# Weight-gradient stores: three half tiles in w1's place for one full tile, and four small rows on GpSimd's queue

## The chip, the cores and the metric

The kernel runs on one core of a Trainium2 chip. The core has five engines that run side by side, each in the order of its own instruction stream: TensorE (PE, with its weight loads shown as PEld), VectorE (DVE), ScalarE (ACT), GpSimd (POOL) and SyncE (SP). Sixteen DMA engines move data between the chip's memory (HBM) and the core's working memory (SBUF); transfers are put on queues by SP, ACT and POOL. Matrix products land in PSUM, of eight banks. The metric is the device time of one execution in microseconds (us), lower is better. Before the change it is 919.31 us, the median of 6 runs (916.63 to 921.01).

## The reference

The reference is one decode step of a transformer block and its gradients. Two sequences (B = 2), one token each, D = 640, 32 heads of 128, caches of 4,096 positions, an MLP with 1,728 hidden units, all in bfloat16.

```python
def _fwd_reference(A_x, A_k_cache, A_v_cache, A_wq, A_wo, B_x, B_w1, B_w2):
    # _A_ref: q = x @ wq; p = softmax(q k^T * Dh**-0.5); o = p v; return o @ wo
    # _B_ref: relu(x @ w1) @ w2
    x = A_x
    h = x + _A_ref(_layernorm(x, axis=-1), A_k_cache, A_v_cache, A_wq, A_wo)
    h2 = h + _B_ref(_layernorm(h, axis=-1), B_w1, B_w2)
    return h2

def reference(...):
    _out, _vjp = jax.vjp(_f, A_x, A_k_cache, A_v_cache, A_wq, A_wo, B_w1, B_w2)
    return (_out, *_vjp(grad_out))
```

There are eight outputs. out_0 is the block's output and out_1 the gradient of x (2 rows of 640 each). out_2 and out_3 are the gradients of the K and V caches, 64 MiB each: per head an outer product of a column over 4,096 positions and a row of 128. out_4 to out_7 are the gradients of wq, wo, w1 and w2: each is a sum of two outer products (one per sequence), 14.9 MB together.

## The kernel before, in words

There are 64 pairs of sequence and head. A first pass (p1_iter) loads K and V of each pair in tiles of 1 MiB (128 partitions of 8 KiB) and makes scores, softmax and attention output. A second pass (p2_iter) needs V once more (tile Wt), makes the gradient of the softmax with it, and writes two outer products of 1 MiB, gK and gV, on VectorE (L829); POOL issues their stores (L867, L886). One call of p2_iter is a turn here; it can be counted by its activation rb (L856). A turn consists of seven steps. In the second half of the second pass there is no first pass beside it.

Beside the turns run three background generators in a fixed program order: bg (the MLP, then go_group, which makes the gradient at the attention output for a group of heads, then mlp_out), bg2 (fin_gen, the weight gradients) and bg3 (gx_gen, the gradient of x). The Python code that builds the program gives each a credit per step (0.65 for bg2), and each `yield` says what a piece costs; nothing is decided at run time. Each engine executes its own instructions in the order in which they were built.

SBUF is handed out in tiles of 8 KiB per partition with tags: "ld" for loads, "g" for gK and gV, "q" for weights late in the kernel, "f" for weight gradients under way. take() gets a tile of a tag and give() brings it back; share() sets how many each tag is to own, and a tile that comes back goes to a tag that owns too few. rested(tag, n) is true when the tag's next tile was given back at least n steps ago. Twelve tiles exist from the start; more come when pools that are no longer needed are released. When the MLP no longer needs w1 (17,280 bytes per partition), its place goes to the pools fin (small tiles of the weight gradients) and big2 (one tile of 8 KiB, tag "f"). Until turn 36 this is the only "f" tile; from then on share() wants three.

outer_rows makes a weight gradient. For each row k of a group and each piece of up to 512 columns, PE makes an outer product into a PSUM tile o_ps (L933), ScalarE copies it into the tile ot (L939), and when the tile is full ScalarE issues its store (L941). One tile holds 4,096 elements per partition: six rows of 640 or two of 1,728 or 2,048. Before it takes a tile, outer_rows waits for rested("f", 13). The order is out_7, out_6, out_5 in two halves, out_4 in two halves.

store_row (L644 on) turns one row of out_0 or out_1 by PE, copies it on VectorE into orow and issues a DMA of 5 x 128 elements, on SP's queue (L651). SP issues the loads of Wt (L458), wqs (L975) and w2 (L361) in program order on the same queue. gx_gen uses a tile gxj of 2 KiB per partition in fin as the place for products that nobody reads.

Of the kernel before, what the change touches and what calls it, by code (L numbers as in the profile page):

```python
# [8 lines left out]
BF16 = mybir.dt.bfloat16  # L9
# [6 lines left out]
def kernel(  # L16
# [20 lines left out]
    nc = tc.nc  # L37

    B, Sq, D = A_x.shape
    _, H, Sk, Dh = A_k_cache.shape  # L40
# [25 lines left out]
    cols = ctx.enter_context(tc.tile_pool(name="cols", bufs=1))  # L66
# [6 lines left out]
    def pst(shape, dtype, role, name):  # L73

        k = banks[role].pop(0)
        banks[role].append(k)
        return ps.tile(shape, dtype, tag=f"bank{k}", bufs=1, name=name)


    NBIG = 12  # L80
    homes = {"ld": list(range(NBIG)), "g": [], "f": [], "q": []}
    free = {tag: len(v) for tag, v in homes.items()}
    owned = dict(free)
    wanted = {}
    pools = [big] * NBIG
# [3 lines left out]
    def take(tag, shape, name):  # L89
        assert free[tag] > 0, (tag, name)  # L90
        free[tag] -= 1
        k = homes[tag].pop(0)
        t = pools[k].tile(shape, BF16, tag=f"big{k}", bufs=1, name=name)
        home_of[id(t)] = (tag, k, t)
        return t

    def goes_to(tag):

        if owned[tag] > wanted.get(tag, len(pools)):
            for other in homes:  # L100
                if owned[other] < wanted.get(other, 0):
                    return other
        return tag

    def give(t, to=None):
        tag, k, _ = home_of.pop(id(t))
        to = to or goes_to(tag)
        owned[tag] -= 1
        owned[to] += 1
        free[to] += 1  # L110
        homes[to].append(k)
        given_at[k] = step[0]

    def rested(tag, n):

        return free[tag] > 0 and (forced[0] or step[0] >= given_at.get(homes[tag][0], -n) + n)

    def share(**want):

        wanted.clear()  # L120
        wanted.update(want)
        for tag in homes:
            while free[tag] > 0 and goes_to(tag) != tag:
                to = goes_to(tag)
                homes[to].append(homes[tag].pop(0))
                for d in (free, owned):
                    d[tag] -= 1
                    d[to] += 1

    def more_home(tag, pool):  # L130
        homes[tag].append(len(pools))
        pools.append(pool)
        free[tag] += 1
        owned[tag] += 1
# [6 lines left out]
    def wait(n):  # L141

        end = step[0] + n * spread[0]
        while step[0] < end and not forced[0]:
            yield 0.0
        yield
# [493 lines left out]
    def spread_cols(t, colsrc, n):  # L640

        for c in range(n):
            nc.tensor.transpose(t[:, c * 128:(c + 1) * 128], colsrc[:, c:c + 1].to_broadcast([128, 128]), ident_bf[:])

    def store_row(col_bf, n, dst):

        t = pst([16, 128], BF16, "mid", "row_ps")
        nc.tensor.transpose(t[0:n, :], col_bf, ident_bf[:])
        r = small.tile([16, 128], BF16, tag="orow", bufs=2, name="orow")
        nc.vector.tensor_copy(out=r[0:n, :], in_=t[0:n, :])  # L650
        nc.sync.dma_start(out=dst, in_=r[0:n, :])  # L651

    def ttr(in0, in1, acc, width, kc=128, junk=None):
        if junk is None:
# [259 lines left out]
    def outer_rows(L, nrow, R, N, out_ap, cc):  # L914


        P = nrow // cc
        grp = max(1, min(cc, 4096 // N))
        out_v = out_ap.rearrange("(p c) n -> p c n", c=cc)
        for c0 in range(0, cc, grp):  # L920
            gn = min(grp, cc - c0)
            while not rested("f", 13):
                yield 0.0
            ot = take("f", [128, grp, N], "ot")
            todo = [(k, n0, min(512, N - n0)) for k in range(gn) for n0 in range(0, N, 512)]
            made = []
            for x in range(len(todo) + 1):
                if x < len(todo):
                    k, n0, nn = todo[x]
                    q = 32 * (fw[0] % 4)  # L930
                    o_ps = pst([128, 512], FP32, "o", "o_ps")
                    fw[0] += 1
                    nc.tensor.matmul(o_ps[0:P, 0:nn], lhsT=L[q:q + B, bass.ds(c0 + k, P, step=cc)],  # L933
                                     rhs=R[q:q + B, n0:n0 + nn], start=True, stop=True)
                    made.append((o_ps, k, n0, nn))
                    yield 0.3
                if x > 0:
                    o_ps, k, n0, nn = made[x - 1]
                    nc.scalar.copy(out=ot[0:P, k, n0:n0 + nn], in_=o_ps[0:P, 0:nn])  # L939
                    yield 0.3  # L940
            nc.scalar.dma_start(out=out_v[:, c0:c0 + gn, :], in_=ot[0:P, 0:gn, :])  # L941
            give(ot)

    def fin_gen(fin):
        FIN["wide"] = [fin.tile([128, 4, 4, 32], BF16, tag="wide", bufs=2, name="wide") for _ in range(2)]
# [23 lines left out]
    def gx_gen(fin):  # L969
        tiles = []  # L970

        def fetch():
            while len(tiles) < ND and free["q"] > 0:
                t = take("q", [128, HD], "wqs")
                nc.sync.dma_start(out=t[:], in_=wq_r[:, len(tiles), :])  # L975
                tiles.append((t, step[0]))

        while not all(("go", B - 1, h) in done for h in range(H)):
            yield 0.0
        while free["q"] < B:  # L980
            yield 0.0
        banks["o"].remove(6)
        banks["gq"] = [6]
        yield from wait(1)
        rows = []
        for b in range(B):
            row = take("q", [128, HD], "gqr")
            for h0 in range(0, H, GH):
                t_ps = pst([128, GH * 128], BF16, "gq", "gq_ps")
                spread_cols(t_ps, GQc[:, h0:h0 + GH, b], GH)  # L990
                nc.scalar.copy(out=row[:, h0 * 128:(h0 + GH) * 128], in_=t_ps[:])
                yield 1.0
            rows.append(row)
        banks["o"].append(6)
        GW = 1024
        NGW = HD // GW
        gxp = fin.tile([128, B, ND, NGW], FP32, tag="gxp", name="gxp")
        junk = fin.tile([128, GW], BF16, tag="gxj", name="gxj")
        for c in range(ND):
            while c >= len(tiles) or (step[0] < tiles[c][1] + 16 and not forced[0]):  # L1000
                fetch()
                yield 0.0
            t = tiles[c][0]
            for b in range(B):
                for k in range(NGW):
                    ttr(t[:, k * GW:(k + 1) * GW], rows[b][:, k * GW:(k + 1) * GW], gxp[:, b, c, k:k + 1], GW, junk=junk)
                    if b == B - 1 and k == NGW - 1:
                        give(t)
                        fetch()
                    yield 0.9  # L1010
        for row in rows:
            give(row)
        gx_bf = fin.tile([128, ND, B], BF16, tag="gxb", name="gx_bf")
        gx1b = fin.tile([128, B, ND], FP32, tag="gx1b", name="gx1b")
        nc.vector.reduce_sum(out=gx1b[:], in_=gxp[:], axis=AX.X)
        yield from ln_bwd(gx1b[:], x1c[:], rstd1[:], gh1c[:], gx_bf[:], B)
        for b in range(B):
            gxo = small.tile([128, ND], BF16, tag="gxo", bufs=2, name="gxo")
            nc.vector.tensor_copy(out=gxo[:], in_=gx_bf[:, :, b])
            yield from wait(2)  # L1020
            store_row(gxo[:], ND, out_1[b].rearrange("s (c p) -> (s c) p", p=128))
            yield
# [94 lines left out]
    fin = big1 = big2 = big3 = None  # L1117
# [12 lines left out]
    for n, (i, j) in enumerate(plan):  # L1130
# [4 lines left out]
        if i is None and plan[n - 1][0] is not None:  # L1135
            pkp.release()
            big1 = tc.alloc_tile_pool(name="big1", bufs=1)
            more_home("ld", big1)
            share(ld=KEPT[1] + 4, g=4)
# [6 lines left out]
        more = int(late[0])  # L1146
        if fin is not None and not bg2 and not bg3:
            share(ld=8 + 3 * more, g=6 + 3 * more)
        elif fin is not None and j >= H + KEPT[1] - 1:
            share(ld=5 + more, g=4 + 2 * more, f=3, q=2 + 3 * more)  # L1150
        if j is not None:
            while g2 is not None:
                p2_step()
# [3 lines left out]
        if i is None and ("w1", 1) in done and fin is None:  # L1157
            wts.release()
            fin = tc.alloc_tile_pool(name="fin", bufs=1)
            big2 = tc.alloc_tile_pool(name="big2", bufs=1)  # L1160
            more_home("f", big2)
            banks.update(sps=[2, 3], o=[4, 5, 6])
            bg2.append(("fin", fin_gen(fin)))
            bg3.append(("gx", gx_gen(fin)))
# [85 lines left out]
```

## Time and profile before

| what | value |
|---|---|
| median of 6 runs | 919.31 us (916.63 to 921.01) |
| the profiled execution | 920.25 us, span 917.9 us |
| PE, DVE, ACT, POOL busy | 745.9, 694.1, 531.4, 167.1 us (81, 76, 58, 18%) |
| bytes moved by DMA | 363.00 MB, mean 395 GB/s |
| queue of the loads (SP), of gK and gV (POOL), of ACT | 212.18, 134.23, 14.91 MB; 57.9, 35.4, 4.1% of 16 engines' span |
| stores of ot | 18, of 432 to 1,024 KB, 323 to 392 ns each to issue, 6.0 to 20.6 us to landing |
| gK and gV stores | 128, 0.53 us each to issue, 5.2 to 30.8 us to landing |
| stores of orow | 4, on SP, 1.2 KB each |
| last instruction of the loop | gK store at 907.4 us |

The span is the time from the first to the last instruction of the profiled execution; its device time lies a little above it. Busy times of engines overlap. A DMA share of 1.0 says that all sixteen engines had packets all the time.

### The profile page before, as it was taken

To read this page: it belongs to the slowest core of one execution; us is meant where nothing else is said; L and a number is where in the kernel's file an instruction comes from. 1 tells how busy PE (TensorE), PEld (TensorE's weight loads), DVE (VectorE), ACT (ScalarE), POOL (GpSimd) and SP (SyncE) were. 2 spreads that over 40 slices of the span, in tenths; PEclk is the share of its full clock that TensorE was granted. 3 is DMA by queue.
4 is the path that set the end of the run, shared out by engine and by line. 5 is a ranking of instruction groups with operands and counts; after the bars stand their busy time and mean duration, and the time that the engine had idled before them with its cause. 6 is when DMAs were issued, how large, how long until landed. Compare 5 with 4: busy or idle time off the path is not lost.

```text
span 917.9 us, 26498 instructions
## 1 busy us (share of the span) xinstructions
PE 745.9 (81%) x11226; PEld 623.5 (68%) x11226; DVE 694.1 (76%) x1291; ACT 531.4 (58%) x1096; POOL 167.1 (18%) x329
## 2 busy tenths in 40 slices
PE   5998998999989898888887827776868799878492
PEld 5887787888878787777776726655757566555362
DVE  4654786877779888777787889878798449998875
ACT  4564554566777777676742626444646667566362
POOL 1222222223201111010011112211122111111111
PEclk9998998999999999999985767555555556565556
DMA  9999999998789999999999999999999999999997
GB/s 346 418 395 410 406 396 409 412 416 338 305 315 332 419 421 422 422 422 421 413 379 425 372 426 397 392 381 411 379 378 386 425 386 425 425 425 425 427 418 301
DMA packets 59478, 363.00 MB, mean 395 GB/s; under 512 B 5696, under 2 KB 15552, under 8 KB 19168
## 3 DMA queue, kind: packets, MB, share of 16 engines
q1 hardware_dynamic: 37920, 212.18, 57.9%
q0 software_dynamic: 18432, 134.23, 35.4%
q10 hardware_dynamic: 3008, 14.91, 4.1%
q8 instruction: 88, 1.44, 0.6%
q14 instruction: 30, 0.25, 0.1%
HBM read 212.16 MB, written 149.13 MB: 394 GB/s over the span
## 4 chain that ended last, share of the span: by engine, by line
PE 37%; DMA 31%; DVE 16%; ACT 8%; issue 6%; POOL 0%; SPq 0%; POOLq 0%; ACTq 0%; DVEq 0%
DMA Vt<-in_A_v_cache_dram 16%; DMA out_dram<-gV 9%; PE t_ps L437 9%; PE m_ps L471 7%; PE t_ps L416 6%; DMA out_dram<-gK 6%; DVE gV L829 4%; ACT t_sb L421 3%; DVE gK L829 3%; PE o_ps L933 3%; PE s_ps L427 3%; DVE junk L656 2%; PE u_ps L500 2%; ACT t_sb L442 2%; PE dp_ps L450 2%
## 5 line engine op out<-in xcount | busy, mean ns | idle before, releaser
L421 ACT COPY t_sb<-t_ps 128x1024 bf16<-128x1024 bf16 x223 | 217.8, 1017 | 49.7 <-PE t_ps L416 49.0
L442 ACT COPY t_sb<-t_ps 128x512 f32<-128x512 f32 x256 | 149.8, 587 | 149.0 <-PE t_ps L437 144.6
L478 DVE TENSOR_TENSOR pk<-Kt,ep 128x2048 bf16<-128x2048 bf16 x128 | 156.4, 1222 | 62.5 <-ACT ep L526 27.1
L437 PE MATMUL t_ps<-ident_f,Wt 128*128 128x128 f32 x848 | 192.6, 374 | 2.6 <-ACT t_sb L421 2.6
L471 PE MATMUL m_ps<-pk,Vt 128*128 128x129 bf16 x2048 | 173.5, 224 | 17.5 <-DMA Vt<-in_A_v_cache_dram 15.9
L829 DVE TENSOR_TENSOR gV<-rb,pp 128x2048 bf16<-128x2048 bf16 x128 | 152.8, 1218 | 22.1 <-DMA out_dram<-gV 16.8
L829 DVE TENSOR_TENSOR gK<-rb,gsp 128x2048 bf16<-128x2048 bf16 x128 | 152.2, 1224 | 19.1 <-DMA out_dram<-gK 17.0
L416 PE MATMUL t_ps<-ident_bf,Kt 128*128 128x128 bf16 x2048 | 153.4, 224 | 8.9 <-DMA Kt<-in_A_k_cache_dram 3.0
L471 PEld LDWEIGHTS <-Vt 128*128 128x128 bf16 x2048 | 126.3, 99 | 49.5 <-issue 30.0
L437 PEld LDWEIGHTS t_ps<-ident_f,Wt 128*128 128x128 f32 x848 | 133.0, 193 | 32.7 <-issue 25.6
L416 PEld LDWEIGHTS <-Kt 128*128 128x128 bf16 x2048 | 125.7, 100 | 15.3 <-issue 9.4
L450 PEld LDWEIGHTS <-t_sb 128*128 128x128 bf16 x2048 | 95.5, 106 | 39.9 <-ACT t_sb L442 19.0
L450 PE MATMUL dp_ps<-gom,t_sb 128*128 128x2 bf16 x2048 | 95.1, 167 | 9.1 <-ACT t_sb L442 8.2
L488 POOL COPY pk<-ep 128x16 bf16<-128x16 bf16 x80 | 63.6, 797 | 193.4 <-ACT ep L526 155.3
L427 PE MATMUL s_ps<-qc,t_sb 128*128 128x1 bf16 x2048 | 88.3, 164 | 1.6 <-DVE t_sb L419 0.8
L867 POOL DMA_DIRECT2D out_dram<-gK x64 | 34.0, 532 | 275.9 <-DVE gK L829 202.6
L886 POOL DMA_DIRECT2D out_dram<-gV x64 | 34.2, 534 | 270.4 <-DVE gV L829 223.2
L427 PEld LDWEIGHTS <-t_sb 128*128 128x128 bf16 x2048 | 78.3, 97 | 4.0 <-ACT t_sb L421 1.2
L939 ACT CAST ot<-o_ps 128x512 bf16<-128x512 f32 (+4 forms) x160 | 70.5, 489 | 15.6 <-DMA out_dram<-ot 8.6
L583 ACT CAST MT<-m_ps 128x128 bf16<-128x128 f32 x64 | 17.1, 267 | 78.9 <-PE m_ps L471 78.8
L856 ACT ACTIVATE rb<-dp_ps,rt 128x256 bf16<-128x256 f32 x64 | 30.3, 474 | 46.6 <-PE dp_ps L851 45.9
L656 DVE CUSTOM_DVE_ANT_0 junk<-wo_t,hbc 128x640 bf16<-128x640 bf16 x64 | 52.3, 818 | 0.2
(194 smaller groups left out, 775.8 us busy)
## 6 DMA issues: line engine op xcount, KB each, us to landing
Kt<-in_A_k_cache_dram SPq DMA_DIRECT2D x64, 1024.0 KB, 13.8
Vt<-in_A_v_cache_dram SPq DMA_DIRECT2D x64, 1024.0 KB, 15.3
out_dram<-gV POOLq DMA_DIRECT2D x64, 1024.0 KB, 11.3
out_dram<-gK POOLq DMA_DIRECT2D x64, 1024.0 KB, 11.0
Wt<-in_A_v_cache_dram SPq DMA_DIRECT2D x53, 1024.0 KB, 12.1
wo_t<-in_A_wo_dram SPq DMA_DIRECT2D x4, 1280.0 KB, 19.7
wqs<-in_A_wq_dram SPq DMA_DIRECT2D x5, 1024.0 KB, 15.8
wq_t<-in_A_wq_dram SPq DMA_DIRECT2D x5, 960.0 KB, 11.2
```

The lines of the kernel that those rows point to most:

```text
L416: nc.tensor.transpose(t_ps[:, j, :], nat[:, g * GT + j, :], ident_bf[:])
L421: nc.scalar.copy(out=t_sb[:], in_=t_ps[:])
L427: nc.tensor.matmul(dst[:, sc:sc + 1], lhsT=t_sb[:, j, :], rhs=vec, start=True, stop=True)
L437: nc.tensor.transpose(t_ps[:, j, :], natf[:, 2 * cc:2 * cc + 2, :].rearrange("p c k -> p (c k)"), ident_f[:])
L442: nc.scalar.copy(out=t_sb[:], in_=t_ps[:])
L450: nc.tensor.matmul(dst[:, sc:sc + 2], lhsT=v[:, j, :, par], rhs=vecs[:, par, :], start=(par == 0), stop=(par == 1))
L471: nc.tensor.matmul(r["m"][:, 0:129], lhsT=r["V"][:, sc, :], rhs=r["pk"][sc // HALF][:, sc % HALF, 0:129], start=(sc == 0), stop=(sc == NSC ...
L478: nc.vector.tensor_tensor(out=p["pk"][k][:, :, 0:128].rearrange("p s (a two) -> p s a two", two=2), in0=p["K"][:, sl, :].rearrange("p s (a ...
L488: nc.gpsimd.tensor_copy(out=col, in_=e)
L656: nc.vector.tensor_tensor_reduce(out=junk[0:kc, 0:width], in0=in0, in1=in1, scale=1.0, scalar=0.0, op0=ALU.mult, op1=ALU.add, accum_out=acc)
L829: nc.vector.tensor_tensor(out=pairs_view(dst[:, sl, :]), in0=row.rearrange("p (a two) -> p a two", two=2)[:, None, :, :].to_broadcast([128 ...
L939: nc.scalar.copy(out=ot[0:P, k, n0:n0 + nn], in_=o_ps[0:P, 0:nn])
```

## The change

A fifth tag "h" is added. big2 gives three tiles to it, which outer_rows fills to 2,048 elements per partition (4 KiB): three rows of 640, or one of 1,728 or 2,048. outer_rows takes a rested "f" tile if there is one, otherwise a rested "h" tile, and the size of the group follows from the tile. share() wants two "f" tiles instead of three, and "h" keeps its tiles. The place for the third half tile comes from gxj, which moves from fin into the place of fbc (a row of the MLP that is no longer needed). store_row issues its DMA from GpSimd.

```diff
-    homes = {"ld": list(range(NBIG)), "g": [], "f": [], "q": []}
+    homes = {"ld": list(range(NBIG)), "g": [], "f": [], "q": [], "h": []}
...
-        if owned[tag] > wanted.get(tag, len(pools)):
+        if tag != "h" and owned[tag] > wanted.get(tag, len(pools)):
...
-        for tag in homes:
+        for tag in ("ld", "g", "f", "q"):
...
-        nc.sync.dma_start(out=dst, in_=r[0:n, :])
+        nc.gpsimd.dma_start(out=dst, in_=r[0:n, :])
...
-        grp = max(1, min(cc, 4096 // N))
         out_v = out_ap.rearrange("(p c) n -> p c n", c=cc)
-        for c0 in range(0, cc, grp):
+        c0 = 0
+        while c0 < cc:
+            while not rested("f", 13) and not rested("h", 13):
+                yield 0.0
+            tag = "f" if rested("f", 13) else "h"
+            grp = max(1, min(cc, (4096 if tag == "f" else 2048) // N))
             gn = min(grp, cc - c0)
-            while not rested("f", 13):
-                yield 0.0
-            ot = take("f", [128, grp, N], "ot")
+            ot = take(tag, [128, grp, N], "ot")
...
             give(ot)
+            c0 += gn
...
-        junk = fin.tile([128, GW], BF16, tag="gxj", name="gxj")
+        junk = cols.tile([128, GW], BF16, tag="fbc", name="gxj")
...
-            share(ld=5 + more, g=4 + 2 * more, f=3, q=2 + 3 * more)
+            share(ld=5 + more, g=4 + 2 * more, f=2, q=2 + 3 * more)
...
-            more_home("f", big2)
+            for _ in range(3):
+                more_home("h", big2)
```

## The prediction

> **What bounds the kernel now.** First the page's second part, in 40 slices of 23 us. The "PEclk" line shows TensorE at about half clock from slice 22 on. The DMA lines say what is full.
>
> ```profile
> PEclk9998998999999999999985767555555556565556
> DMA  9999999998789999999999999999999999999997
> GB/s 346 418 395 410 406 396 409 412 416 338 305 315 332 419 421 422 422 422 421 413 379 425 372 426 397 392 381 411 379 378 386 425 386 425 425 425 425 427 418 301
> ```
>
> The 16 DMA engines are over 90% busy in all slices but three and the last. Full speed looks like 425 GB/s, and slices 34 to 38 hold it. So bytes count, and time is lost only where the engines pause or move less than 425. Second, the table of windows over the stretch in which the weight gradients are made (columns: window, length, busy time and count of PE, PEld, DVE, ACT, POOL, then granted clock, DMA share, GB/s).
>
> ```profile
> 590.00:610.00 20.00, 10.48 (x98) 7.93 (x95) 13.53 (x24) 7.80 (x18) 2.17 (x7) 0.58 0.99 391
> 610.00:620.00 10.00, 9.09 (x86) 7.90 (x86) 8.19 (x18) 4.85 (x11) 2.01 (x5) 0.50 0.94 335
> 640.00:645.00 5.00, 5.00 (x47) 4.34 (x47) 4.79 (x14) 3.70 (x10) 1.31 (x3) 0.50 0.94 329
> 670.00:675.00 5.00, 0.74 (x6) 0.56 (x6) 4.49 (x7) 1.05 (x2) 1.79 (x3) 0.68 0.93 389
> 675.00:680.00 5.00, 2.97 (x29) 2.39 (x28) 4.90 (x9) 1.17 (x2) 1.25 (x2) 0.50 0.73 301
> 680.00:690.00 10.00, 9.97 (x79) 6.88 (x76) 9.79 (x21) 7.32 (x15) 1.84 (x4) 0.50 0.98 393
> 705.00:870.00 165.00, 128.28 (x1134) 94.54 (x1131) 128.94 (x175) 97.89 (x211) 23.93 (x51) 0.55 1.01 420
> 895.00:905.00 10.00, 6.07 (x96) 4.85 (x94) 9.93 (x11) 5.16 (x10) 2.62 (x6) 0.95 0.98 401
> 905.00:910.00 5.00, 0.00 (x0) 0.00 (x0) 2.08 (x2) 0.00 (x0) 0.84 (x2) 0.50 1.00 411
> ```
>
> From 705 to 895 us the queues never run dry, whatever the engines do. Before that, one minus the share, times the length, gives 0.2 + 0.6 + 0.3 + 0.35 + 1.35 + 0.2 = 3.0 us of idle DMA. At the end 401 and 411 instead of 425 lose 0.56 + 0.16 = 0.7 us.
>
> Third, the timeline of ScalarE around the first stores of out_7, made of one 8 KiB tile.
>
> ```profile
> 584.01 0.39 ACTq L941 DMA_DIRECT2D out_dram<-ot  x1
> ...
> 598.96 0.58 ACT L939 CAST ot<-o_ps 96x512 bf16<-96x512 f32 x1 [6.47 <-DMA out_dram<-ot]
> ...
> 626.62 0.58 ACT L939 CAST ot<-o_ps 96x512 bf16<-96x512 f32 x1 [2.10 <-DMA out_dram<-ot]
> ```
>
> The next row needs the tile whose store is still under way, and ScalarE stands 6.47 and 2.10 us, with the t_sb copies of the main loop behind it.
>
> Last, the waits of SP's queue.
>
> ```profile
> SPq L651 <- DVE gxo L1019: 35.8, 1, 35.8
> SPq L651 <- DVE orow L650: 16.4, 3, 10.2
> ```
>
> These are the small rows. The 35.8 us lie after the last load was issued (848 us), so nothing is behind them. The 10.2 us hold two loads back at 808 us, where DMA is full.
>
> **The Trainium skill.** "Trainium Kernel Development and Optimization", Key Constraints: the DMAs of the SP, ACT and POOL queues run on the same 16 engines, and issuing from several saves only sequencer time. The trace agrees: loads, gradient stores and weight-gradient stores together move 425 GB/s and not more. "DMA: Bandwidth & Descriptors", Queues, rings and completion order: an engine takes the queue rows in turn, a packet at a time. That fits the 15 us that the first store of 720 KB needed, with loads and gK/gV stores beside it.
>
> **The change part by part.** I count turns of the second pass by the rb activation (L856); the program order of both kernels can be laid side by side.
>
> *Half tiles.* Until turn 36 the old kernel has one "f" tile, so it rests 13 steps after every store. The new one has three half tiles in turn. Out_7 ended at turn 34 and ends at 31; out_6 at 40, now 37; the last store of out_4 at 61, now 58. Bytes, matmuls and copies (160 of them) stay the same. Stores go from 18 to 25: 7 x 0.345 us = 2.4 us of ScalarE issue, hidden, since ScalarE is 58% busy and waits for PE. In the trace's packets 6,912 bytes took 262 ns and 3,456 took 138, so halving costs 14 ns: 256 packets of out_6 x 14 / 16 engines = 0.2 us; out_7's 288 packets of 7,680 bytes (291 ns) become twice as many of 3,840, about 150 ns interpolated, another 0.2. With the completion writes (7 stores x 16 x 9 ns / 16 = 0.06) the full DMA pays **+0.5 us**.
>
> *What earlier stores fill.* Moving a byte where DMA is full saves nothing; it must go into the 3.0 us of idle. Most lies at 670 to 690. There the queue has no loads (the next five V tiles of batch 1 were kept), out_6's 864 KB store of 666 us has delayed the gV store that DVE needs until 674.8, PE waits 5.1 us in order for goc behind that gV, and the queue runs empty. In the new order out_6 is done by turn 37, in a stretch where loads are still queued, so those loads reach into the pause, and no weight store stands in front of gV at turns 38 to 40. The two ScalarE stands go: a half tile comes back after two others, and its store is half as long. Bounds: 0 (the pause moves) to 3.0 (all filled). I take **-2.2**, three quarters.
>
> *The end.* Turns 58 to 61 took about 9 us each (rb at 871.25, 880.04, 889.93), PE alternating t_ps and o_ps at half clock, while DMA had 2 MB of gradients (4.9 us) and some 2 us of out_4 per turn, so the backlog drained. At 895 to 910 it was thin. With out_4 over at turn 58 the last six turns run at 4.9 us (rb 894.75, 898.61; gK and gV need 4 x 1.2 us of DVE). Six "g" tiles keep DMA full. Bounds 0 to 0.7; I take **-0.7**, since nothing else is in those turns.
>
> *Rows from POOL.* Four issues leave SP and enter POOL's queue, with 1.2 KB each. A gradient store there took 0.53 us, so 2.1 us in all on an engine 18% busy. Behind the rows of out_0 stands a gV store, behind those of out_1 a gV and a gK store, and these wait for DVE work that comes later than orow on DVE, so the row costs no wait. Uncovered it would be 2 us once. On SP the loads come up to 10 us earlier, into a full DMA: nothing. I take 0; the ends are -0.3, if the loads freed at 808 us fill some gap after all, and +1, if half of the issue time is on the path.
>
> *junk in fbc's place.* DVE writes and never reads it; its earlier users ended before turn 30. 0. Neither the tiles of "ld", "g" and "q" nor the order of their transfers changes: wanted f is 3 with w1's tile, or 2 without it.
>
> The sum is +0.5 - 2.2 - 0.7 + 0 = **-2.4 us**. The profiled execution took 920.25 us (span 917.9 and 2.35 around it), so 917.85 for it; it was 0.94 above the median of 919.31, which gives **916.9**. This kernel's runs (916.63 to 921.01) tell some 0.2%, or 1.8 us, from no change.
>
> **The rivals.**
> *Hidden anyway (no change).* DMA conserves bytes. If the pause just moves to turns 38 to 40, where now no weight store is at hand, the gain is the end's 0.7 less 0.5: 919.1. For it: 98% of the span is DMA. Against it: the idle has a named cause.
> *A starved stretch (slower).* At 662 to 704 no load is queued. A turn without weight work took 5.3 us (rb at 615.73 and 621.02) against 4.9 us of DMA for its two gradients; with goc and rows in it 6 to 7.7. If turns 38 to 41 run with gK and gV alone at 6.5 us, DMA idles 1.6 x 4 = 6.4 us where it idled 1.9, +4.5 in place of -2.2: -2.4 + 6.7 = +4.3, or 923.6; half of it 921.4. It decides once the loads put off by out_6 (2.2 MB, 5.2 us) are used up before turn 39. For it: the share falls to 0.73 the one time nothing is queued. Against it: out_5 starts at turn 41, not 44, and refills the stretch.
> *The stands were on the path (larger gain).* If each us of ScalarE's 8.6 delays a gradient store that DMA lacked, then the 8.6 go in full: 912. Against it: the share was 0.99 during the first.
>
> **How the numbers follow.** Forecast 0.45 (915.5 to 918.3, a quarter of it within 0.2%), no change 0.23, starved 0.22, larger gain 0.10. Faster: 0.34 + 0.10 = 0.44, and 0.01 from the edges of the others; same: 0.11 + 0.19 = 0.30; slower: 0.20 + 0.05 for row stores that do stall POOL or slow packets in a new mix (read packets at 750 us took some 1.6 us more than their median without a cause that I see). The range 913.8 to 921.8 leaves out the deep ends of the second and third rival.
>
> **What would show it.** Right: 25 stores from ScalarE, the last about 875 us; no wait of ot for its own store above 1 us; the share at 670 to 690 above 0.95; 420 GB/s or more until the last gradient. Wrong: shares under 0.9 at turns 38 to 41 (starved); the same 3 us of idle elsewhere (no change); gV or gK stores on POOL waiting for orow; SP loads waiting for a store of ot.

## The result: slower by 0.6%, and where the time went

The changed kernel took 924.05 us (median of 18 runs, 921.22 to 928.84), the kernel before 918.81 us (median of 39, 915.29 to 927.26): a ratio of 1.0057, with a 95% interval of 1.0038 to 1.0075, or +5.2 us. The forecast of 916.9 us had the wrong sign, and the range ended at 921.8. What came true is the rival called a starved stretch, which was priced at 923.6 us.

The page of the kernel after, slices of 23 us as before:

```profile
PEclk9999998999999999999985867556555655656576
DMA  9999999998789999999999999999997999999997
GB/s 347 418 396 409 407 394 409 412 414 348 289 306 337 407 410 423 423 423 419 420 386 397 380 426 400 393 392 409 403 389 294 424 418 426 421 425 425 424 411 310
```

Slice 31 (the one from 691 to 714 us) moves 294 GB/s, and its DMA digit is 7; the kernel before had 386 and 9 there. The table of windows of the kernel after for the stretches that the prediction had chosen (columns: window, length, busy time and count of PE, PEld, DVE, ACT, POOL, then granted clock, DMA share, GB/s):

```profile
590.00:610.00 20.00, 17.58 (x132) 12.60 (x133) 13.13 (x23) 11.86 (x29) 2.61 (x6) 0.50 1.01 383
610.00:620.00 10.00, 6.89 (x65) 5.80 (x65) 7.62 (x17) 4.44 (x11) 1.30 (x3) 0.50 1.02 405
640.00:645.00 5.00, 4.16 (x31) 2.76 (x30) 4.85 (x13) 2.15 (x5) 1.01 (x3) 0.50 0.98 406
670.00:675.00 5.00, 3.90 (x44) 3.45 (x42) 4.18 (x8) 2.80 (x7) 0.90 (x3) 0.50 1.02 425
675.00:680.00 5.00, 1.38 (x11) 1.05 (x10) 4.93 (x10) 1.36 (x4) 1.11 (x2) 0.50 0.96 401
680.00:690.00 10.00, 6.84 (x67) 5.57 (x66) 7.55 (x17) 3.91 (x8) 2.56 (x5) 0.50 0.91 375
690.00:695.00 5.00, 4.68 (x32) 2.79 (x30) 5.00 (x8) 2.55 (x7) 0.53 (x1) 0.50 0.37 152
695.00:700.00 5.00, 4.55 (x33) 2.82 (x33) 2.55 (x4) 3.70 (x10) 0.77 (x2) 0.50 0.70 288
700.00:705.00 5.00, 5.00 (x41) 3.78 (x40) 4.32 (x7) 3.21 (x8) 0.85 (x2) 0.50 0.80 328
710.00:870.00 160.00, 125.21 (x1150) 90.21 (x1150) 123.66 (x169) 98.25 (x208) 23.02 (x49) 0.59 1.01 423
895.00:905.00 10.00, 6.46 (x100) 5.23 (x98) 9.93 (x11) 5.44 (x10) 3.60 (x6) 0.91 0.99 402
905.00:910.00 5.00, 0.00 (x0) 0.00 (x0) 4.61 (x5) 0.00 (x0) 1.13 (x3) 0.50 1.01 415
```

The gaps that the prediction wanted to fill are smaller, up to 680 us: shares of 0.99, 0.94, 0.94, 0.93 and 0.73 became 1.01, 1.02, 0.98, 1.02 and 0.96. A part of that is only that the turns come some microseconds later: turn 39, which holds the largest of these gaps, still idles 1.1 us, against 1.8 before. Behind them a larger one opened. One minus the share, times the length, is 0.9 + 3.15 + 1.5 + 1.0 = 6.55 us from 680 to 705 us. The same table of the kernel before shows next to nothing after 690:

```profile
690.00:695.00 5.00, 4.79 (x53) 4.08 (x52) 4.52 (x7) 3.70 (x10) 2.28 (x3) 0.50 1.00 409
695.00:700.00 5.00, 3.06 (x45) 2.73 (x43) 4.17 (x10) 2.71 (x7) 0.77 (x2) 0.84 0.99 339
700.00:705.00 5.00, 4.39 (x48) 4.12 (x47) 4.47 (x10) 3.20 (x8) 0.57 (x2) 0.50 1.00 358
```

What is missing there is seen on the queues. ScalarE's timeline of the kernel after, only the rows of its stores, from 655 to 706 us:

```profile
659.23 0.34 ACTq L943 DMA_DIRECT2D out_dram<-ot  x1
663.08 0.34 ACTq L943 DMA_DIRECT2D out_dram<-ot  x1
...
700.19 0.34 ACTq L943 DMA_DIRECT2D out_dram<-ot  x1
```

The same rows of the kernel before, from 655 to 730 us:

```profile
666.06 0.37 ACTq L941 DMA_DIRECT2D out_dram<-ot  x1
...
686.60 0.36 ACTq L941 DMA_DIRECT2D out_dram<-ot  x1
...
691.71 0.34 ACTq L941 DMA_DIRECT2D out_dram<-ot  x1
...
726.30 0.34 ACTq L941 DMA_DIRECT2D out_dram<-ot  x1
```

And SP's timeline of the kernel after, in which a row joins two issues of the same line with the pause between them:

```profile
657.90 46.69 SPq L458 DMA_DIRECT2D Wt<-in_A_v_cache_dram  x2
704.64 0.95 SPq L361 DMA_DIRECT2D w_t<-in_B_w_dram  x1
```

From 663 to 700 us nothing is issued but gK and gV. The loads pause in both kernels (before from 654 to 696 us), since after turn 36 share() hands four tiles of the loads to other tags; before, three stores of weight gradients stood in that pause.

Set out by stages of turns (length, bytes moved, and idle of DMA, that is the length less the packets' time over 16 engines, summed over the turns in which it is positive):

| turns | before | after | difference |
|---|---|---|---|
| start to 26 | 569.8 us | 572.2 us | +2.4 us |
| 27 to 36 | 85.3 us, 33.2 MB, idle 0.8 | 88.2 us, 35.1 MB, idle 0.4 | +2.9 us |
| 37 to 42 | 50.8 us, 19.5 MB, idle 2.0 | 55.7 us, 19.8 MB, idle 6.6 | +4.9 us |
| 43 to 46 | 45.3 us, 18.4 MB, idle 0.1 | 39.2 us, 16.5 MB, idle 0.0 | -6.1 us |
| 47 to 58 | 103.0 us, 43.7 MB, idle 0.0 | 107.5 us, 45.6 MB, idle 0.0 | +4.5 us |
| 59 to the end | 63.7 us, 24.1 MB | 58.0 us, 21.7 MB | -5.7 us |

The sum of the differences is that of the spans (920.9 and 917.9 us). The first row lies in the first pass, ahead of the first weight-gradient store of both kernels. Of the nine profiled executions with half tiles, eight reached turn 27 at 571.4 to 575.6 us and one (e10 below) at 570.2; the five with full tiles did so at 569.8 to 570.3. What makes this difference is not shown; it isn't what decides the time, since e7, e9 and e11, at 571.4 to 572.7, end level with the kernel before. Of the rest, every stage but one roughly follows its bytes. Turns 27 to 36 pay for the stores that came earlier, with DMA full; turns 37 to 42 move the same bytes and last 4.9 us longer. These 4.6 us of additional idle are of the size of the loss, which is 3.0 us between these two executions and 5.2 us between the medians. Counted over the whole span, the packets took 900.5 us after and 901.0 before, so that DMA stood idle for 20.5 and for 16.8 us: what grew is the idle, not the work of DMA.

### The profile page after: what moved, and what is told of

It is laid out like the page before. It is cut to its first block, busy times and chain, and to the rows that moved or that the text cites. A ratio compares the mean times of both kernels' runs of the same rounds, so it can differ in the third digit from the quotient of the medians.

```text
span 920.9 us, 26503 instructions
## 1 busy us (share of the span) xinstructions
PE 742.5 (81%) x11226; PEld 616.4 (67%) x11226; DVE 693.2 (75%) x1291; ACT 531.6 (58%) x1096; POOL 170.6 (19%) x333
## 4 chain that ended last, share of the span: by engine, by line
PE 34%; DMA 28%; DVE 22%; ACT 8%; issue 6%; POOL 0%; SPq 0%; POOLq 0%; DVEq 0%; ACTq 0%
DMA Vt<-in_A_v_cache_dram 14%; DMA out_dram<-gV 9%; PE m_ps L471 8%; PE t_ps L416 7%; DVE gV L829 6%; PE t_ps L437 6%; DMA out_dram<-gK 5%; DVE gK L829 5%; ACT t_sb L421 4%; DVE gxj L656 3%; PE s_ps L427 3%; PE u_ps L500 3%; DVE junk L656 2%; DVE pk L478 2%; ACT t_sb L442 2%
## 5 line engine op out<-in xcount | busy, mean ns | idle before, releaser
L437 PE MATMUL t_ps<-ident_f,Wt 128*128 128x128 f32 x848 | 187.1, 366 | 2.8 <-ACT t_sb L421 2.8
L829 DVE TENSOR_TENSOR gK<-rb,gsp 128x2048 bf16<-128x2048 bf16 x128 | 152.1, 1223 | 23.6 <-DMA out_dram<-gK 21.7
L829 DVE TENSOR_TENSOR gV<-rb,pp 128x2048 bf16<-128x2048 bf16 x128 | 152.8, 1218 | 19.5 <-DMA out_dram<-gV 17.0
L437 PEld LDWEIGHTS t_ps<-ident_f,Wt 128*128 128x128 f32 x848 | 129.6, 189 | 30.0 <-issue 16.5
L450 PEld LDWEIGHTS <-t_sb 128*128 128x128 bf16 x2048 | 92.9, 105 | 44.9 <-ACT t_sb L442 22.1
L427 PEld LDWEIGHTS <-t_sb 128*128 128x128 bf16 x2048 | 78.2, 97 | 3.7 <-DVE t_sb L419 1.3
L583 ACT CAST MT<-m_ps 128x128 bf16<-128x128 f32 x64 | 17.1, 266 | 78.1 <-PE m_ps L471 78.0
## 6 DMA issues: line engine op xcount, KB each, us to landing
wo_t<-in_A_wo_dram SPq DMA_DIRECT2D x4, 1280.0 KB, 19.5
wqs<-in_A_wq_dram SPq DMA_DIRECT2D x5, 1024.0 KB, 20.5
```

Of the source, the lines that this page charges most:

```text
L427: nc.tensor.matmul(dst[:, sc:sc + 1], lhsT=t_sb[:, j, :], rhs=vec, start=True, stop=True)
L437: nc.tensor.transpose(t_ps[:, j, :], natf[:, 2 * cc:2 * cc + 2, :].rearrange("p c k -> p (c k)"), ident_f[:])
L450: nc.tensor.matmul(dst[:, sc:sc + 2], lhsT=v[:, j, :, par], rhs=vecs[:, par, :], start=(par == 0), stop=(par == 1))
L829: nc.vector.tensor_tensor(out=pairs_view(dst[:, sl, :]), in0=row.rearrange("p (a two) -> p a two", two=2)[:, None, :, :].to_broadcast([128 ...
```

## The experiments

Each was timed beside the kernel before on the same chip; ratios are to that. The kernel before took 917.95 us beside e1 to e4, 918.75 beside e5 to e8, 918.27 beside e9 and e10, and 917.57 beside e11 and e12, so the medians of different groups don't compare to the microsecond. Idle is counted as in the table above, in one execution each. The kernel before, e1 and e3 have their weight stores in the same turns and yet show 2.0, 0.9 and 0.1 us in turns 37 to 42, so a difference of less than 2 us says little.

| label | median | ratio, 95% interval | idle, turns 37 to 42 | 43 to 46 | 59 to 63 |
|---|---|---|---|---|---|
| before | 918.81 us | | 2.0 us | 0.1 us | 0.1 us |
| after | 924.05 us | 1.0057 (1.0038 to 1.0075) | 6.6 us | 0.0 us | 0.2 us |
| e1_rows_only | 918.22 us | 0.9998 (0.9979 to 1.0016) | 0.9 us | 0.3 us | 0.1 us |
| e2_halves_only | 924.54 us | 1.0078 (1.0049 to 1.0107) | 6.7 us | 0.0 us | 0.0 us |
| e3_split_stores | 918.28 us | 1.0009 (0.9992 to 1.0027) | 0.1 us | 1.4 us | 0.0 us |
| e4_hold36 | 925.24 us | 1.0085 (1.0058 to 1.0112) | 0.9 us | 5.8 us | 0.0 us |
| e5_qlate_after | 919.80 us | 1.0008 (0.9987 to 1.0029) | 3.1 us | 0.0 us | 0.0 us |
| e6_qlate_before | 920.18 us | 1.0017 (1.0000 to 1.0035) | 0.7 us | 3.5 us | 0.0 us |
| e7_no_f_tiles | 919.28 us | 0.9998 (0.9981 to 1.0014) | 2.7 us | 0.0 us | 0.7 us |
| e8_hold37 | 924.91 us | 1.0059 (1.0044 to 1.0075) | 0.5 us | 5.1 us | 0.2 us |
| e9_hold_and_loads | 919.16 us | 1.0009 (0.9992 to 1.0027) | 0.2 us | 0.1 us | 3.6 us |
| e10_hold_both | 917.15 us | 0.9984 (0.9969 to 1.0000) | 0.2 us | 0.0 us | 3.1 us |
| e11_order_after | 917.52 us | 0.9997 (0.9984 to 1.0011) | 0.3 us | 0.0 us | 0.0 us |
| e12_order_before | 917.43 us | 1.0003 (0.9980 to 1.0025) | 0.8 us | 0.0 us | 0.0 us |

### Which part of the change

The theory after the result: the stores have come too early, and the queue runs empty in turns 39 to 41. Rivals: POOL's row stores are in the way, or the smaller transfers are dear. e1 is the kernel before with only the rows moved:

```diff
-        nc.sync.dma_start(out=dst, in_=r[0:n, :])
+        nc.gpsimd.dma_start(out=dst, in_=r[0:n, :])
```

> The kernel before with the four small rows issued from GpSimd, nothing else. Starved-stretch theory (the weight stores of out_6 are over at turn 37, before loads run out, and turns 39 to 41 leave DMA with nothing but gK and gV): 0 us against before, at most 1. Rival rows (a gradient store on GpSimd stands behind a row): most of the 5.2 us. Rival small stores: 0.

e2 is the changed kernel with that line as it was before:

```diff
-        nc.gpsimd.dma_start(out=dst, in_=r[0:n, :])
+        nc.sync.dma_start(out=dst, in_=r[0:n, :])
```

> The changed kernel with the rows issued from SP again. Starved stretch: +4 to +6 us against before (about 924), the idle DMA of turns 39 to 41 some 6 us, as in the changed kernel. Rival rows: 0. Rival small stores: +5.

e3 is the kernel before, in which each full tile is filled at its old place and stored by two transfers:

```diff
-            nc.scalar.dma_start(out=out_v[:, c0:c0 + gn, :], in_=ot[0:P, 0:gn, :])
+            for k0 in range(0, gn, max(1, grp // 2)):
+                kn = min(max(1, grp // 2), gn - k0)
+                nc.scalar.dma_start(out=out_v[:, c0 + k0:c0 + k0 + kn, :], in_=ot[0:P, k0:k0 + kn, :])
```

> The kernel before, its 8 KiB tile kept, but each full tile stored by two transfers of half the size, issued one after the other at the same place: the sizes and the count of the stores change, their turns do not. Starved stretch: +0 to +1 us, since out_6 is still stored at turns 38 and 40. Rival small stores (packets, issues and completions of halves cost time wherever they stand): +4 to +5.

The rows alone gave 0.9998, the split stores alone 1.0009, and the half tiles without the rows 1.0078, the whole loss. So neither rival holds. e3 has the small transfers, and their place in the order is what it was: size is cleared, and the place remains. The windows of e2 show the same hole as those of the changed kernel:

```profile
690.00:695.00 5.00, 4.68 (x35) 2.71 (x34) 4.74 (x11) 2.84 (x8) 0.53 (x1) 0.50 0.36 146
695.00:700.00 5.00, 4.55 (x39) 3.23 (x40) 2.58 (x5) 3.46 (x9) 0.77 (x2) 0.50 0.76 315
700.00:705.00 5.00, 5.00 (x35) 3.52 (x34) 4.90 (x9) 3.12 (x8) 0.53 (x1) 0.50 0.74 301
```

### Putting out_6 back: e4

If out_6's early end makes the hole, holding out_6 must close it. The turn's number is noted where p2_iter is called (jnow counts from 0, so 36 is turn 37):

```diff
+        while jnow[0] < 36 and not forced[0]:
+            yield 0.0
         yield from outer_rows(FIN["x2r"], D, FIN["ghfr"], Dff, out_6, ND)
```

> The changed kernel, but the first row of out_6 waits for turn 37, so that its stores go out at turns 37, 37, 38 and 40 and those of out_5 from turn 44 on. Starved stretch: the idle of turns 39 to 41 falls from 6.4 us to 2 or less, and the time to that of before or 2 below it (916.5 to 919.5). Rival small stores: it stays at 924.

The hole in turns 39 to 41 closed (idle of turns 37 to 42: 0.9 us), and the kernel was as slow as before that edit, 925.24 us, because another opened five turns later. The windows of e4 are its turns 44, 45 and 46:

```profile
719.70:735.20 15.50, 10.49 (x82) 7.38 (x81) 4.46 (x5) 7.86 (x16) 1.30 (x3) 0.50 0.91 362
735.20:746.80 11.60, 10.39 (x106) 7.96 (x106) 5.12 (x7) 7.58 (x16) 1.30 (x3) 0.50 0.63 221
746.80:756.00 9.20, 6.84 (x59) 5.09 (x58) 4.84 (x6) 5.26 (x13) 1.30 (x3) 0.50 0.99 402
```

The miss says that "the early store of out_6 costs 5 us" is no whole account. The first hole is confirmed as out_6's; a second place lies near the edge.

### Filling the hole with loads: e5, e6, e7

The pause of the loads is made by share(). e5 keeps the order of the stores of the changed kernel, and leaves the loads the two tiles that gx_gen isn't yet using, so that two loads of Wt come in turns 39 and 40:

```diff
-            share(ld=5 + more, g=4 + 2 * more, f=2, q=2 + 3 * more)
+            share(ld=7 - more, g=4 + 2 * more, f=2, q=5 * more)
```

> The changed kernel, in which the two q tiles that loads give up at turns 39 and 40 stay with the loads until turn 43 (share ld=7, q=0 before, the old numbers from then on). Weight stores keep their turns; two loads of 1 MB move into turns 39 and 40. Starved-queue theory (what the change costs is DMA idle in turns 39 to 45, where TensorE sets the pace and loads pause): the idle of turns 39 to 41 falls from 6.4 to some 2 us, and the time to 919 to 922. Rival early contention (the stores at turns 27 to 37 slow the gradients there, and that is what is lost): no change from 924.

e6 makes the same edit in the kernel before:

```diff
-            share(ld=5 + more, g=4 + 2 * more, f=3, q=2 + 3 * more)
+            share(ld=7 - more, g=4 + 2 * more, f=3, q=5 * more)
```

> The same move of two loads in the kernel before. Its idle there is 1.8 us in the profile of before. Starved queue: 0.5 to 2 us faster than before. Rival early contention: 0.

e7 takes the two tiles from "f" instead, so that all weight gradients from turn 36 on go by half tiles:

```diff
-            share(ld=5 + more, g=4 + 2 * more, f=2, q=2 + 3 * more)
+            share(ld=7 + more, g=4 + 2 * more, f=0, q=2 + 3 * more)
```

> The changed kernel without f tiles (share f=0, ld=7): all stores are half tiles, the loads keep the two tiles, so that loads come at turns 39 and 40 and the first store of out_5 at turn 40, the last store of out_4 at turn 60. Starved queue: the idle of turns 39 to 41 falls below 2 us, time 917 to 921. Rival small stores: slower than 924. Rival early contention: 924.

In time e5 and e7 came out as expected: 919.80 and 919.28 us, level with the kernel before, while every store of out_7 and out_6 is as early as in the changed kernel. The idle of turns 39 to 41 fell less than expected, from 6.4 us to 3.1 in e5 and 2.2 in e7, where some 2 and below 2 were said; the kernel before has 1.9 there. The windows of e7 at the place of the hole:

```profile
690.00:695.00 5.00, 5.00 (x43) 3.61 (x42) 4.87 (x10) 3.03 (x8) 0.53 (x1) 0.50 0.99 331
695.00:700.00 5.00, 4.60 (x38) 2.84 (x35) 3.19 (x6) 3.75 (x9) 0.78 (x2) 0.50 1.05 374
700.00:705.00 5.00, 5.00 (x41) 3.89 (x39) 4.76 (x8) 3.15 (x8) 0.53 (x1) 0.50 0.96 324
```

Two loads in two turns bring shares of 0.37, 0.70 and 0.80 to 0.99, 1.05 and 0.96. So it isn't the early store that costs, but that nothing is queued for the turns that it left. One more thing differs there: in turns 40 and 41 of the changed kernel ScalarE copies 8 and 7 pieces of weight gradients (out_5 has begun), in the kernel before 6 and none, so TensorE has more to do just where nothing is queued. e7 keeps these 8 and 7 pieces and closes the hole with bytes. What the pieces add to the hole was not tried: no run holds out_5 and leaves out_6 early.

e6 missed: 920.18 us where 0.5 to 2 us less than before was expected. It too has a second hole, 3.5 us in turns 43 to 46. Two loads had been moved forward, and here, with out_5's pieces in turns 43 to 45, they were probably missed there; no run tried that by itself. Even the kernel before is near the edge at this place: e3, which has its order, idles 1.4 us there.

### The second hole: e8, e9, e10

e8 holds out_6 for one turn more than e4, which puts all stores from turn 41 to 44 into the turns that they have in the kernel before.

```diff
-        while jnow[0] < 36 and not forced[0]:
+        while jnow[0] < 37 and not forced[0]:
```

> The changed kernel with out_6 held until turn 38, so that from there on all weight stores stand at the turns of before (38 to 40, 44 to 47, 50 to 52, 56, 57, 60, 61); only out_7 is early. Starved queue: idle of turns 39 to 41 under 1 us as with the hold one turn earlier; whether turns 44 and 45 run empty again shows if that second hole belongs to out_5 standing one turn off. If it does not come back, 917 to 920; if it does, 923 to 926.

The second hole stayed: 0.5 us of idle in turns 37 to 42, 5.1 in turns 43 to 46, 924.91 us. By the start of turn 41 e8 and the kernel before had issued the same loads and the same 4.4 MB of weight gradients. Three turns, 43 to 45, took 40.6 us in e8 and 36.2 before, and in 40.6 us DMA could have moved 17.2 MB, more than was queued. Two readings were left: the turns are long because TensorE makes out_5's pieces among the transposes of gq, or bytes are missing. e9 and e10 take the two apart. e9 is e8 with the edit of e7, both fillers, each for one hole; against e8:

```diff
-            share(ld=5 + more, g=4 + 2 * more, f=2, q=2 + 3 * more)
+            share(ld=7 + more, g=4 + 2 * more, f=0, q=2 + 3 * more)
```

> The changed kernel with both fillers: out_6 held until turn 38 (as in the hold to turn 38 before) and no tile taken from the loads for f (f = 0, ld = 7, so that two loads stand in turns 39 and 40). Theory of the thin queue (each hole opens where the bytes at hand run out, and either filler gives bytes at its own place): out_6 fills turn 39, the two loads carry 2 MB over turns 43 to 45, so the idle of turns 37 to 46 is under 1.5 us in all and the time 917.5 to 919.5, some 5 us under the changed kernel and level with the kernel before (difference within 1.5 us). Rival 'a hold always costs' (holding the stores makes TensorE's turns 43 to 45 longer, and that alone costs, whatever is queued): the turns 43 to 45 stay at 38 to 41 us together with idle of 4 us or more, 923 to 925. Rival 'bytes moved to the end' (the half tiles now end at turn 63): DMA idle in turns 58 to 64 of 2 us or more, 921 to 923.

e10 is e8 with out_5 held too, which takes its pieces out of turns 43 to 45 and its stores with them:

```diff
+        while jnow[0] < 45 and not forced[0]:
+            yield 0.0
         yield from rows_of(fin, gh1c, ND, "gh1r", "rD")
```

> The changed kernel with out_6 held until turn 38 and out_5 (its rows, its pieces and its stores) held until turn 46, so that TensorE has none of the o_ps pieces (8 a turn, about 3.5 us at half clock) in turns 43 to 45 beside the gq transposes. Theory 'TensorE's turns drain the queue' (in the run with out_6 held until turn 38 the turns 43 to 45 were 40.6 us long for 12.6 MB of gradients and 3 to 5 MB of loads, and the missing bytes were missing because the turns were long): turns 43 to 45 fall to 30 us or less in all, the idle there from 5 us to under 2, time 919 to 921.5. Rival 'the bytes are missing' (out_7's were stored early, and with out_5's first 1 MB of turn 44 and its second of turn 45 gone too there is nothing to move): the idle at turns 43 to 46 stays at 4 us or more, 924 or more.

The windows of e8 are its turns 43, 44 and 45:

```profile
706.50:721.60 15.10, 10.73 (x85) 8.25 (x83) 5.36 (x7) 8.38 (x18) 1.31 (x3) 0.50 1.01 428
721.60:734.10 12.50, 10.50 (x82) 7.30 (x81) 4.49 (x5) 7.82 (x17) 1.31 (x3) 0.50 0.94 360
734.10:747.10 13.00, 10.16 (x105) 7.84 (x104) 5.11 (x7) 7.45 (x16) 1.31 (x3) 0.50 0.67 251
```

The same three turns of e10:

```profile
699.90:707.80 7.90, 6.56 (x79) 5.69 (x78) 4.83 (x6) 5.65 (x8) 1.79 (x3) 0.77 1.01 423
707.80:713.70 5.90, 4.59 (x74) 4.01 (x74) 3.59 (x4) 5.27 (x10) 0.77 (x2) 1.00 1.01 421
713.70:719.20 5.50, 4.56 (x94) 4.11 (x94) 2.88 (x5) 4.35 (x8) 0.77 (x2) 1.00 1.02 428
```

With two stores fewer in these turns, not more, the hole is gone: turns of 19.3 us in all in place of 40.6, DMA full throughout. The missing bytes were missing because the turns were too long for what was queued. (The six gradient stores that e8 issues in these turns are 6.3 MB, not the 12.6 of the expectation.) The groups of TensorE's instructions say how out_5's pieces do that (22 of them are in the trace); first e8 over its three turns (columns: line, operation, names, shapes, count, busy us and mean ns, idle just before them and what ended it):

```profile
L437 PE MATMUL t_ps<-ident_f,Wt 128*128 128x128 f32 x50 | 13.6, 424 | 0.0
L643 PE MATMUL gq_ps<-ident_bf,GQc 128*128 128x128 bf16 x64 | 8.3, 310 | 0.5 <-ACT ot L942 0.5
L936 PE MATMUL o_ps<-gh1r,OFr 2*128 2x512 bf16 x11 | 6.7, 609 | 5.7 <-ACT ot L942 5.7
...
L936 PE MATMUL o_ps<-gh1r,OFr 2*128 2x128 bf16 x11 | 3.1, 282 | 3.1 <-ACT ot L942 2.9
```

Then e10 over its own:

```profile
L437 PE MATMUL t_ps<-ident_f,Wt 128*128 128x128 f32 x50 | 8.9, 312 | 0.0
L643 PE MATMUL gq_ps<-ident_bf,GQc 128*128 128x128 bf16 x64 | 5.3, 229 | 2.2 <-ACT gqr L999 2.2
```

The pieces themselves are 9.8 us, TensorE stands 8.8 us ahead of them, nearly all of it for ScalarE to empty their banks, and the other work runs slower around them: a transpose of Wt takes 424 ns against 312, at a granted clock of 0.50 against 0.77 to 1.00. e10 takes out the pieces, the waits for their banks and the low clock together; it doesn't say how much each of them adds.

e9 agrees from the other side: with two more loads at hand the turns stay long (36.5 us, and 36.2 in the kernel before) and idle only 0.1 us; 919.16 us lies in the range of the theory. Its rival about the end was right in the idle, 3.6 us in turns 59 to 63, since its stores go on to the last turn, but not in the 921 to 923 us. e10, which also ends late, idles 3.1 us there, and yet it has the lowest ratio; its 917.15 us are 2 us below what had been expected. A part of that lies behind turn 63: in the last turn e10 idles 2.4 us and the kernel before 6.0. Over the whole span it is 13.7 against 16.8 us, in one execution each.

### A version without holes: e11, e12

e11 is e8 with out_5 held until turn 44 and a higher credit for the weight gradients behind that, so that they end at turn 59:

```diff
+        while jnow[0] < 43 and not forced[0]:
+            yield 0.0
         yield from rows_of(fin, gh1c, ND, "gh1r", "rD")
...
-                bg_step(1, RATE2)
+                bg_step(1, RATE2 if j is None or j < 45 else 0.9)
```

> A version meant to beat both: the changed kernel with out_6 held until turn 38, out_5 held until turn 44 (so that no o_ps piece and no store falls in turns 41 to 45, as in the run that held both), and the credit of the weight gradients raised from 0.65 to 0.9 a step from turn 45 on, so that the last store comes at turn 59 and not at turn 64. Theory of the queue that drains: turns 41 to 45 stay under 8 us each with DMA idle under 0.5 us in turns 37 to 46, the backlog of 6 to 8 MB at turn 47 covers the longer TensorE turns of 47 to 58, and turns 60 to 64 have gK and gV alone at 5 us, idle under 1 us in place of 3 to 4 us in the run that held both: 913.5 to 916.5. Rival 'the end always pays' (the weight gradients cost TensorE some 3.5 us a turn wherever they stand, and DMA runs dry behind the last of them): idle of 3 us or more in turns 58 to 62, 917 to 919.

e12 makes these two edits in the kernel before, with its full tiles and its places of out_7 and out_6:

```diff
+        while jnow[0] < 43 and not forced[0]:
+            yield 0.0
...
+                bg_step(1, RATE2 if j is None or j < 45 else 0.9)
```

> The kernel before with the same order from turn 41 on: full tiles, out_7 and out_6 where they were, out_5 held until turn 44 and the credit 0.9 from turn 45. Theory 'what counts is when the pieces and bytes of the weight gradients come, not the size of the tiles': level with the version of the changed kernel in the same order, within 1.5 us, but for up to 1.5 us more idle in turn 39: 914 to 917.5. Rival 'the half tiles bring the gain once their order is mended': 918 or more here, and 2 us or more above the version with half tiles.

Both orders did what they were built for: idle of 0.3 and 0.8 us from turn 37 to 63. And neither beat the kernel before (0.9997 and 1.0003); e11 missed its 913.5 to 916.5 us by a microsecond. e11 and e12 are level with each other, so the size of the tiles brings nothing in this order either. The windows of e11 at its end:

```profile
886.00:905.00 19.00, 7.75 (x98) 6.56 (x96) 15.08 (x16) 5.63 (x10) 5.21 (x9) 0.68 1.01 417
905.00:910.00 5.00, 0.00 (x0) 0.00 (x0) 0.00 (x0) 0.00 (x0) 0.00 (x0) 0.50 0.64 267
910.00:914.00 4.00, 0.00 (x0) 0.00 (x0) 0.00 (x0) 0.00 (x0) 0.00 (x0) 0.50 0.06 25
```

Its last gK store is issued at 902.1 us, 5.3 us before that of the kernel before (907.4), but lands 11.8 us later, behind what is still queued (before 8.8 us). Of 5.3 us, 2.2 us are left in this one execution (spans of 915.7 and 917.9 us) and none in the medians. The kernel before idles some 3 us from turn 27 to 63; that is all that an order of these turns could win back, and it is not much above what a measurement can tell. Another 6.0 us lie in its last turn. Of the versions only e10 is below the kernel before, by 0.16% with an interval that touches 1, so it isn't shown to beat it.

## Why the prediction was wrong

**Half tiles, +0.5.** Not contradicted. e3 pays the transfers alone: +0.8 us by its ratio, -0.7 to +2.5 by the interval. The count of 25 stores was right, and so were their turns (out_7 to 31, out_6 to 37, out_4 to 58). The time of the last one was not: turn 58 begins at 851 us, and it was issued at 855.6, not about 875.

**What earlier stores fill, -2.2.** This is the step that failed; measured it is +4.6 us of idle. Its rule was right: a byte that moves where DMA is full saves nothing and must go into idle. The bytes went into turns 27 to 36 instead, where idle was 0.8 us, and lengthened these by 2.9 us. The sentence "those loads reach into the pause" carried the gain, and it had no number. It took the loads to be put off by all of the 2.2 MB. But the turns ahead were as long as their DMA, so most of these bytes were paid there by longer turns: at the start of turn 38 the queue (bytes issued less bytes moved, without the instructions' own) was 1.0 MB ahead of the kernel before, 3.0 against 2.0 MB; at turn 39 it was level, 1.8 against 1.7; at turn 40 it was down to 0.3 MB, against 1.4. The pause lost 2.2 MB and got 1.0. The rival had named the test, whether what out_6 put off is used up before turn 39, and the trace of before had the parts for it: turns 38 to 41 lasted 35.4 us, at TensorE's pace, with 10.5 MB of gradients in them, 24.7 us at 425 GB/s, and no load to fill the rest before 696 us. Not done, that sum left the rival at 0.22. "Out_5 starts at turn 41, not 44, and refills the stretch" was true and too late: its first store is at 700.2 us, and its pieces came ahead of it, into turns 40 and 41, where they gave TensorE more work before DMA got a byte of them.

Two smaller statements of that step held. PE's wait for goc behind a late gV fell from 5.1 to 3.6 us in turns 39 and 40. And the stands of ScalarE are gone. Of ScalarE's waits in the kernel after, these rows are for ot (what waited, for what: us in all, times, the longest):

```profile
ACT ot L941 <- PE o_ps L935: 13.6, 11, 7.0
ACT ot L941 <- ACT ot L941: 1.8, 4, 0.5
ACT ot L941 <- PE dp_ps L450: 0.9, 2, 0.5
```

None is for a store; before, two waits for stores made 8.6 us. 8.6 us of stands went, and the kernel lost 5. That alone doesn't refute the third rival, that they were on the path, since the hole came at the same time. e11 and e12 do: with the same order from turn 41 on, ScalarE stands 11.1 us for stores of ot in e12 (full tiles) and not at all in e11 (half tiles), and the two are level. So 8.6 us of stands weren't 8.6 us of the path.

**The end, -0.7.** Zero. The turns became as short as said (4.8, 5.3, 5.0 and 3.9 us for turns 60 to 63), but the rates did not follow: 402 and 415 GB/s in the two windows in place of 401 and 411. One reading of that step doesn't hold in the trace of before: turns 58 to 61 took 10.7, 17.1, 8.8 and 9.9 us, not about 9 each; DMA idled in none of them. Nor did the backlog grow with out_4 gone: at the start of turns 62 and 63 it was 0.8 and 0.9 MB after and 1.6 and 1.7 before, at nearly the same rates. So the lower rate there has another cause than the backlog; which, no run here shows.

**Rows from POOL, 0.** Right within the noise: 0.9998 in e1. The four issues took 0.51 us each.

**The rivals.** The starved stretch was right in its place and its sign. Its price of +4.3 supposed 6.5 us for each of turns 38 to 41; the idle came in turns 39 to 41, of 14.9, 8.9 and 8.0 us. Its sign for the wrong case, shares under 0.9, is there: 0.52 in turn 40 and 0.87 in 41. A side price of the chances was misread: from 740 to 760 us the longest read packet took 1.17 us, 0.86 above the median of 0.31, not 1.6.

What stays open: turn 43 took 15.1 us in e8 against 12.0 before, with 8 pieces in place of 7; TensorE stood 3.9 us there for copies of ot and 1.4 before, but why these come late was not followed further. And the idle of turns 37 to 63 explains the losses of 5 us and more, not the rest to the microsecond: e11 idles 2 us less there than the kernel before and isn't faster.

## What to carry to other kernels

In this kernel, where DMA is the bound, a store that came earlier was a loan: it cost its time at once, and was paid back only where its old place found other bytes in the queue. So before a transfer is moved out of a stretch, add up what is left for that stretch (stores, and loads that have a free tile) and set it against the stretch's length at the pace of its slowest engine. And where a hole opens, look at both sides: two loads of 1 MiB filled it here, and so did taking work off the engine that made the turns long.

## What the runs showed of the hardware

A small share of TensorE's work went together with a halved clock: without out_5's outer products in three turns (43 to 45 of e10) the granted clock was 0.77 to 1.00, with them (e8) 0.50, and the same 64 transposes of gq took 229 ns each, not 310. e11 and e12, whose turns 43 to 45 are free of them too, had 0.80 to 1.00 there. They can't be all of it: turns 41 and 42 of e10 are free of them as well and stood at 0.50. The Trainium skill ("TensorE: Matmul & The Clock Gate", Part 1: The HAM clock gate) says that a gate passes half or all of TensorE's clock pulses by how busy TensorE has been of late. Busy time alone doesn't tell these turns apart: TensorE was busy for 71 to 84% of each in e8 and for 78 to 83% in e10. Whether the 8.8 us of stands ahead of these products held the clock at half, no run here tried by itself. Halving the stores' packets to 3,456 to 4,096 bytes cost nothing that can be measured (1.0009). And the last stores don't end at full pace in most of these runs: e11 issued its last one, of gK, at 902.1 us, and from 910 to 914 us DMA ran at a share of 0.06, which is what one engine of sixteen would show. e10, whose last store is one of ScalarE's at 908.6 us, has no such end: DMA is full to 911 us, and nothing is moved from 912 us on. Why the ends differ is open.
